# Attention scores from two 32 bit parts, two heads side by side in the array

## The chip, the core and the metric

The kernel runs on one core of a Trainium2 chip. The metric is the device time of one execution in microseconds (us). A core has a matrix engine (TensorE, PE in the profile, with its weight loads as PEld), a vector engine (VectorE, DVE), a scalar engine (ScalarE, ACT), a general engine (GpSimd, POOL), and DMA queues, which SyncE (SP) and ScalarE issue to here. Every engine works through its own instructions in order and waits for others by semaphores. TensorE writes to eight PSUM banks of 128 rows of 512 32 bit words; VectorE and ScalarE read them there.

## The reference

One transformer block on 2048 tokens of width 512: a layer norm with scale and shift from a condition vector, attention, a gated residual, a second layer norm, an MLP of width 1792 with GELU, a gated residual. The attention has 32 heads of width 16 and works on four segments of 512 tokens. Inside a segment it is causal softmax attention; beside that, a linear memory carried over the segments is read. Cut to the part that the change touches:

```python
logits = jnp.einsum("bhqd,bhkd->bhqk", qs, ks) * scale + mask   # scale 1/4, mask -1e9 above the diagonal
p = _softmax(logits, axis=-1)
a_dot = jnp.einsum("bhqk,bhkd->bhqd", p, vs)
...
o = g * a_mem + (1.0 - g) * a_dot
```

q and k are scaled such that the logits are large, so the maximum of a row has to be subtracted before the exponential, and the products need more than bf16 accuracy.

## The kernel before

The program has three stages. First the projections of q, k and v and the memory, for all four segments; then the scores, with the output projection and the second layer norm mixed in; then the MLP. An explicit order fixes every engine's sequence.

**Operands of the scores.** `proj` (L488) splits q and k, each 128 x 512 for eight heads, into three bf16 parts, and `store` writes them to DRAM as six terms: the six products of parts that matter. `load_stacks` (L177) brings four heads (a *quartet* Q of 32) back as `qst` and `kst`, 96 rows (six terms of 16 dimensions) x 4 heads x 512 positions. One product over 96 rows then gives a score to nearly 32 bit accuracy. Four pairs of buffers rotate (`NK`).

**Two passes over the scores.** A step P handles one pair of heads (64 steps, two per quartet).
- S (`s_part`, L624): scores with queries in rows, for the maxima, in blocks i = 3, 2, 1, 0 of 128 queries with 512, 384, 256 and 128 keys. Parts S0 and S1 take two single banks each, one per head, and `masked_max` (L618, a custom VectorE instruction) adds the causal mask and takes the maximum. S2 and S3 put both heads in one bank; for the last block the mask is added by a product with an identity (`s_mask`, L658, token M3) and one reduction (L622) takes both heads' maxima. S runs four steps (`LEAD`) ahead of T.
- `m_rows` (L671, GpSimd) splits a quartet's negative maxima into three bf16 parts, `m_put` (L677) transposes them on PE (L679) into the bank `mm`, copies them out on ACT and writes them with one DMA, issued by ACT, as rows 96 to 98 of `qst`; `kst` has ones there.
- T (`st_part`, L706): scores transposed, keys in rows, over 99 rows (L700), so that the maximum is already subtracted; ACT takes the exponential from PSUM to `pt` (L715, L726), GpSimd cuts above the diagonal (`causal`, L703). T0 to T3 take a bank per head, T4 and T5 one for both.
- `pv_part` (L740): the values' product, four heads in four 32-column strips of the array, once per key block j for a quartet.

**Order.** The rows of `PRM['order']` give a step's sequence, one row for even and one for odd steps of each segment. S0 to S3, M3 and T0 to T5 are the parts above; c0 to c9 are slots, and a table (`ap`, position 10 x step + slot) puts everything else there: loads of stacks (`stacks`), `m_rows`, `m_put`, value products (`pv`), output projection (`wo_part`, L817), its residual and the layer norm. Six single banks `att` are handed out in turn; one bank is `pv`, one `mm`.

## Time and profile before

| | us |
|---|---|
| median of three runs | 805.82 (804.58 to 812.59) |
| the profiled execution | 803.54 |
| its span | 801.8 |
| granted TensorE clock, mean | 0.994 |

| line | what | count | busy us |
|---|---|---|---|
| L611 | S products, parts 0 to 2 | 384 | 94.3 |
| L700 | T products | 512 | 106.8 |
| L740 | value products | 992 records | 88.2 |
| L618 | masked maxima on DVE | 384 | 192.3 |
| L622 | maxima by reduction on DVE | 64 | 27.2 |
| L715, L726 | exponentials on ACT | 384 | 183.3 |
| L703 | causal cuts on POOL | 256 | 101.9 |

Busy time of a group is the time in which at least one of its instructions ran. PE's records overlap, since a product's end is modelled and the next starts before it; what a product costs in a row of products is the distance of starts, which the chain of work gives. The score stage lasts from about 185 to 490 us of the span.

### The profile page before, as it was taken

To read this page: it belongs to the slowest core of one execution; us is meant where nothing else is said; L and a number is where in the kernel's file an instruction comes from. 1 tells how busy PE (TensorE), PEld (TensorE's weight loads), DVE (VectorE), ACT (ScalarE), POOL (GpSimd) and SP (SyncE) were. 2 spreads that over 40 slices of the span, in tenths; PEclk is the share of its full clock that TensorE was granted. 3 is DMA by queue.
4 is the path that set the end of the run, shared out by engine and by line. 5 is a ranking of instruction groups with operands and counts; after the bars stand their busy time and mean duration, and the time that the engine had idled before them with its cause. 6 is when DMAs were issued, how large, how long until landed. Compare 5 with 4: busy or idle time off the path is not lost.

```text
span 801.8 us, 14163 instructions
## 1 busy us (share of the span) xinstructions
PE 782.6 (98%) x4585; PEld 532.0 (66%) x4585; DVE 557.9 (70%) x1411; ACT 464.9 (58%) x912; POOL 336.2 (42%) x556
## 2 busy tenths in 40 slices
PE   9999999999999999999999998989999999999998
PEld 4877777876444455445544555768888888888887
DVE  6686697459888877697778779866659866533423
ACT  3465545465778766675678574757745336653221
POOL 1347366451478555567866586133000404400000
PEclk9999999999999999999999999999999999999999
DMA  9597857495565676768557854584575644445443
GB/s 339 183 318 233 284 181 233 149 331 170 147 195 164 187 209 174 219 179 216 155 175 203 233 160 147 173 283 155 192 255 176 195 136 158 158 145 171 156 134 117
DMA packets 108818, 156.10 MB, mean 195 GB/s; under 512 B 16324, under 2 KB 55620, under 8 KB 108744
## 3 DMA queue, kind: packets, MB, share of 16 engines
q1 hardware_dynamic: 106248, 153.23, 60.7%
q10 hardware_dynamic: 2496, 1.97, 0.8%
q8 instruction: 36, 0.59, 0.3%
q14 instruction: 38, 0.31, 0.1%
HBM read 93.95 MB, written 60.83 MB: 193 GB/s over the span
## 4 chain that ended last, share of the span: by engine, by line
PE 76%; ACT 7%; DMA 6%; DVE 6%; issue 3%; POOL 1%; SPq 1%; ACTq 0%; DVEq 0%; POOLq 0%
PE pv L740 8%; PE bx L1059 7%; PE att L700 7%; PE att L611 6%; PE q L318 5%; PE bx L1324 5%; PE by L1324 4%; PE bv L1324 4%; PE k L318 4%; PE mm L817 4%; PE bv L1059 4%; PE v L469 3%; DMA qst<-ms 2%; PE spare L1324 2%; ACT pt L715 2%
## 5 line engine op out<-in xcount | busy, mean ns | idle before, releaser
L618 DVE CUSTOM_DVE_ANT_0 dump<-att,maskb 128x512 bf16<-128x512 f32 (+2 forms) x384 | 192.3, 553 | 27.0 <-PE att L611 24.8
L715 ACT ACTIVATE pt<-att 128x512 f32<-128x512 f32 (+1 forms) x256 | 126.1, 558 | 47.0 <-PE att L700 44.3
L703 POOL TENSOR_SCALAR_AFFINE_SELECT pt<-pt 128x256 f32<-128x256 f32 x256 | 101.9, 416 | 82.5 <-ACT pt L715 51.6
L700 PE MATMUL att<-qst,kst 99*128 99x512 bf16 (+3 forms) x512 | 106.8, 301 | 5.6 <-DMA qst<-ms 3.5
L611 PE MATMUL att<-kst,qst 96*128 96x512 bf16 (+2 forms) x384 | 94.3, 327 | 1.7 <-DMA qst<-QD 1.4
L740 PE MATMUL pv<-pt,V 128*32 128x512 f32 (+2 forms) x992 | 88.2, 446 | 0.0
L854 POOL TENSOR_TENSOR wb<-wa 128x256 f32<-128x256 f32 x24 | 21.0, 876 | 154.9 <-DMA wa<-in_w 148.9
L700 PEld LDWEIGHTS <-kst 99*128 99x128 bf16 x512 | 42.9, 97 | 57.6 <-issue 38.7
L726 ACT ACTIVATE pt<-att 128x512 f32<-128x512 f32 (+1 forms) x128 | 57.2, 514 | 21.6 <-PE att L611 19.6
L611 PEld LDWEIGHTS <-qst 96*128 96x128 bf16 x384 | 33.2, 98 | 40.7 <-issue 23.8
L141 DVE TENSOR_TENSOR gl<-s,gh 128x512 fp32r<-128x512 f32 x34 | 24.5, 721 | 42.0 <-ACT gh L138 42.0
L138 ACT ACTIVATE gh<-s 128x512 fp32r<-128x512 f32 x34 | 21.3, 628 | 47.2 <-PE spare L1324 17.1
L740 PEld LDWEIGHTS pv<-pt,V 128*32 128x32 f32 x992 | 22.1, 108 | 36.4 <-issue 26.1
L622 DVE TENSOR_REDUCE nm<-att 128x2 f32<-128x256 f32 x64 | 27.2, 425 | 22.1 <-PE att L658 17.7
L1064 ACT ACTIVATE s<-s,b1t 128x512 f32<-128x512 f32 x42 | 30.2, 720 | 18.6 <-DVE s L1068 18.6
L1068 DVE TENSOR_TENSOR s<-bv,s 128x512 f32<-128x512 f32 x28 | 19.2, 688 | 25.5 <-PE bv L1059 20.2
L618 DVE DVE_READ_ACCUMULATOR2_ANT nm<- 128x1 f32 x384 | 31.9, 83 | 0.0
L514 POOL TENSOR_TENSOR q<-qr,q 128x512 bf16<-128x512 f32 x16 | 18.7, 1167 | 26.7 <-ACT q L513 26.3
L505 POOL TENSOR_SCALAR qp<-qp 128x512 f32<-128x512 f32 x12 | 19.1, 1594 | 24.0 <-ACT qp L500 24.0
L141 DVE TENSOR_TENSOR w1ml<-s,w1mh 128x512 fp32r<-128x512 f32 x18 | 13.0, 721 | 21.5 <-ACT w1mh L138 21.5
L318 PE MATMUL q<-Ahh,wqh 128*128 128x512 f32 x64 | 25.9, 405 | 0.4 <-DVE Ahh L140 0.4
L138 ACT ACTIVATE w1mh<-s 128x512 fp32r<-128x512 f32 x18 | 11.3, 628 | 25.6 <-PE spare L1324 13.1
(364 smaller groups left out, 2112.7 us busy)
## 6 DMA issues: line engine op xcount, KB each, us to landing
GD<-s SPq DMA_DIRECT2D x56, 256.0 KB
s<-GD SPq DMA_DIRECT2D x52, 256.0 KB
kst<-KD SPq DMA_DIRECT2D x32, 384.0 KB
qst<-QD SPq DMA_DIRECT2D x32, 384.0 KB
TD<-ts SPq DMA_DIRECT2D x32, 256.0 KB
xt<-X2D SPq DMA_DIRECT2D x28, 256.0 KB
wa<-in_w SPq DMA_DIRECT2D x28, 256.0 KB
QD<-q SPq DMA_DIRECT2D x16, 384.0 KB
```

Source lines behind the costliest of these rows:

```text
L138: act.activation(hi, src, AF.Copy)
L141: lo_eng.tensor_tensor(out=lo, in0=src, in1=hi.bitcast(F32), op=ALU.subtract)
L318: pe.matmul(ps, a[:, k, 128 * g:128 * g + 128], b[k], start=(k == 0 and i == 0), stop=(k == KB - 1 and i == 2))
L611: pe.matmul(ps, q_of(P, h, i), k_of(P, h, 128 * (i + 1)), start=True, stop=True)
L618: v.tensor_tensor_reduce(out=dump[n_dump[0] % 2][:, :n], in0=src, in1=maskb[:, 512 - n:], scale=-1.0, scalar=-4 * NEG, op0=ALU.add, op1=AL ...
L700: pe.matmul(ps, k[:99, e, 128 * j:128 * j + 128], q[:99, e, 128 * j:512], start=True, stop=True)
L703: pool.affine_select(out=t, in_=t, pattern=pattern, compare_op=ALU.is_ge, fill=0.0, base=0, channel_multiplier=-1)
L715: act.activation(pt[:, h, :], ps[:, :n], AF.Exp, scale=0.25)
L726: act.activation(pt, pv_, AF.Exp, scale=0.25)
L740: pe.matmul(ps[32 * c:32 * c + 32, lo:hi], V[4 * s + j][:, VW * hd:VW * hd + 32], pt[:, c % 2, lo - o:hi - o], start=start, stop=stop)
L1059: pe.matmul(ps, a[:, i, k, :], b[k], start=start and k == 0 and c == 0, stop=k == 1 and c == 2, skip_group_check=not start)
L1324: pe.matmul(ps, a[:, c], w[:, lo:hi], start=(f == 0 and i == 0), stop=(last and i == 2))
```

## The change

- **Operands.** q and k are split into two 32 bit parts (type `float32r`) in place of three bf16 parts; three terms in place of six, 48 rows per head. The bytes in DRAM stay. A head of a pair stands in rows 0 to 47 or 64 to 111 of `qst` and `kst` (now 128 x 2 x 512), its three maxima in the rows behind (48 to 50, 112 to 114). `load_stacks` issues four DMAs per quartet in place of two, `m_put` two in place of one.
- **Banks.** Three pairs of banks `att` in place of six single ones; one head of the pair writes to each bank. A step takes six turns: three S parts (blocks 3; 2 and 0; 1) and three T parts (blocks 0; 1 and 3; 2).
- **Mask.** All blocks get the mask by products: for each head two products over 64 rows, each adding the mask for 64 of the 128 queries (`hid`, `hmask`). The custom maximum is gone; a plain reduction takes both heads at once.
- **Exponentials** run over both heads and both banks: 1024, 1024 and 512 columns.
- **Order.** One sequence for all steps; loads of stacks four slots later; output projection in other slots. In the first stage, a copy on ACT and a subtraction on GpSimd per projection fall away.

```diff
-PRM = {'order': ['S0 c0 c1 T0 T1 S1 c2 T2 c3 c4 c5 T3 S3 c6 M3 S2 c7 c8 c9 T4 T5',
-           'T0 S0 c0 c1 c2 S1 c3 T2 T3 T1 S2 c4 c5 T4 S3 M3 T5 c6 c7 c8 c9',
...
+ORDER = 'S0 T0 S1 c0 c1 c2 c3 c4 T1 S2 c5 c6 c7 c8 c9 T2'
...
- 'stacks': -64,
+ 'stacks': -60,
...
- 'wo': [[2, 10, 10, 10], [6, 10, 11, 11], [2, 10, 10, 11]],
+ 'wo': [[2, 6, 10, 10], [2, 6, 10, 10], [2, 6, 10, 10]],
...
+    TERMS = {"q": (slice(0, 3, 2), slice(1, 2)), "k": (slice(0, 2), slice(2, 3))}
...
-            d[i] = (pl or wmp).tile([128, 4, 512], BF16, **a)
+            d[i] = (pl or wmp).tile([128, 2, 512], F32R, **a)
...
-            sp.dma_start(st[:96], dd[s][g].rearrange("c r e n -> (c r) e n")[:, 4 * t:4 * t + 4, :])
+            for h in range(2):
+                e = 4 * t + 2 * h
+                sp.dma_start(st[64 * h:64 * h + 48].bitcast(F32), dd[s][g].rearrange("c r e n -> (c r) e n")[:, e:e + 2, :])
...
+    v.memset(hid, 0.0)
+    v.memset(hmask, NEG)
+    for t, op, fill in ((hid, ALU.not_equal, 1.0), (hmask, ALU.is_gt, 0.0)):
+        for h in range(2):
+            r = slice(64 * h, 64 * h + 64)
+            pool.affine_select(out=t[r], in_=t[r], pattern=[[-64, 2], [1, 128]], compare_op=op, fill=fill,
+                               base=0, channel_multiplier=-1)
...
-            v.tensor_tensor(out=r1, in0=ps, in1=parts[0], op=ALU.subtract)
+            v.tensor_tensor(out=parts[1], in0=ps, in1=parts[0].bitcast(F32), op=ALU.subtract)
...
-            act.activation(parts[1], r1, AF.Copy)
-            pool.tensor_tensor(out=parts[2], in0=r1, in1=parts[1], op=ALU.subtract)
...
-                 for n, c in (("att", 6), ("pv", 1))}
+                 for n, c, d in (("att", 3, [2, 512]), ("pv", 1, [512]))}
...
+        SP_, TP = ((3,), (2, 0), (1,)), ((0,), (1, 3), (2,))
...
+            ps, lo = bank("att"), 0
+            for c, i in enumerate(SP_[part]):
                 n = 128 * (i + 1)
                 for h in range(2):
+                    pe.matmul(ps[:, h, lo:lo + n], q_of(P, h, i), k_of(P, h, n), start=c == 0, stop=False,
+                              skip_group_check=True)
+                lo += n
+            w = 128 * len(SP_[part])
+            o = lo - 128 if w == 128 else 256
+            for a in range(2):
                 for h in range(2):
+                    r = slice(64 * h, 64 * h + 64)
+                    dst, m = ps[:, h, o:o + w], hmask[r, a]
...
+                    pe.matmul(dst, hid[r, a], m, start=False, stop=a == 1, skip_group_check=True)
+            lo = 0
+            for i in SP_[part]:
                 n = 128 * (i + 1)
+                v.tensor_reduce(out=nms[Q][:, 0:8:4, 4 * p + i], in_=ps[:, :, lo:lo + n], axis=AX.X, op=ALU.max,
+                                negate=True)
+                lo += n
...
         def q_of(P, h, i):
-            return qst[P // 2 % NK][:96, 2 * (P % 2) + h, 128 * i:128 * i + 128]
+            return qst[P // 2 % NK][64 * h:64 * h + 48, P % 2, 128 * i:128 * i + 128]
...
+            ms = sb.tile([64, 128], F32R, tag="ms", bufs=2, name=f"ms{Q}")
+            copy(PRM["mse"], ms, mm[:64, :128])
+            for h in range(2):
+                act.dma_start(qst[Q % NK][64 * h + 48:64 * h + 51].bitcast(F32), ms[32 * h:32 * h + 24].bitcast(F32))
...
         def st_part(P, part):
+            js = TP[part]
+            w = 256 if part == 2 else 512
             ps = bank("att")
+            pt = late[0].tile([128, 2, w], F32, tag=f"pt{part}", bufs=(3, 4, 4)[part], name=f"pt{P}_{part}")
+            lo = 0
+            for j in js:
                 n = 512 - 128 * j
                 for h in range(2):
+                    st_mm(ps[:, h, lo:lo + n], P, h, j)
+                pts[P, j] = pt[:, :, lo:lo + n]
+                lo += n
+            act.activation(pt, ps[:, :, :w], AF.Exp, scale=0.25)
+            for j in js:
+                causal(pts[P, j][:, :, 0:128], [[0, 2], [1, 128]])
```

How the order moves, at two places. First PE in the second segment, from a quartet's transposition of maxima (L679 before, L650 now, from `nm`) to the S products of the next step. Tiles carry a number; `att` are the banks. Before:

```order
L679 MATMUL mm<-identb,nm_2056 128x128
L700 LDWEIGHTS kst_1838
L700 MATMUL att_2063<-qst_1837,kst_1838 128x256 [waits DVE_49]
...
L700 MATMUL att_2064<-qst_1837,kst_1838 128x128 [waits DVE_49]
...
L700 MATMUL att_2065<-qst_1837,kst_1838 128x512 [waits Activation_49]
L611 LDWEIGHTS qst_2138
L611 MATMUL att_2066<-kst_2139,qst_2138 128x512 [waits Activation_49]
```

The change:

```order
L650 MATMUL mm<-identb,nm_1910 128x128
L672 MATMUL att_1919<-qst_1714,kst_1715 128x256 [waits DVE_49]
...
L616 MATMUL att_1917<-kst_1939,qst_1938 128x512 [waits Activation_49]
...
L672 MATMUL att_1918<-qst_1714,kst_1715 128x512 [waits DVE_49]
...
L616 MATMUL att_1919<-kst_1939,qst_1938 128x384 [waits Activation_49]
```

The banks now return after three turns: the last row, S1 of the next step, takes the pair 1919 that T2 took in the second row, and waits for ACT to have read it.

Second, ACT at the same kind of place, around the copy of the maxima (`ms`). Before:

```order
L715 ACTIVATE pt_1_4170<-att_2066 128x384 [waits PE_49]
L132 ACTIVATE ms_4193<-mm 48x128 [waits DMAHW4_49,PE_49]
L682 DMA qst_2075<-ms_4193 3x16x128 [waits DMAHW3_49,Activation_49]
L726 ACTIVATE pt_2_4196<-att_2063 128x512 [waits DVE_49,PE_49]
L726 ACTIVATE pt_3_4201<-att_2064 128x256 [waits DVE_49,PE_49]
```

The change:

```order
L691 ACTIVATE pt_1_4656<-att_1917 128x1024 [waits DVE_49,PE_49]
L124 ACTIVATE ms_4674<-mm 64x128 [waits DMAHW0_49,PE_49]
L654 DMA qst_1721<-ms_4674 3x8x128 [waits DMAHW6_49,Activation_49]
L654 DMA qst_1721<-ms_4674 3x8x128 [waits DMAHW1_49]
L691 ACTIVATE pt_2_4679<-att_1919 128x512 [waits PE_49]
```

Between the exponentials of two T parts stand now a copy and two DMA issues, where one issue stood.

128 lines of the change are left out of this document (34 added, 94 removed), and 8 rows, old and new, of the table PRM.

## The prediction

> **What bounds the kernel now.** I read the page first: the busy line, to see which engine has no time left.
>
> ```profile
> span 801.8 us, 14163 instructions
> PE 782.6 (98%) x4585; PEld 532.0 (66%) x4585; DVE 557.9 (70%) x1411; ACT 464.9 (58%) x912; POOL 336.2 (42%) x556
> ```
>
> TensorE (PE) is covered for 98% of the span. An average hides stages, so the second view was the busy time by stretches, and for the score stage the same view for line L648 alone, which runs once per step (a step is one pair of heads, 64 in all).
>
> ```profile
> 60.00:100.00 40.00, 40.00 (x181) 29.58 (x180) 25.41 (x47) 21.55 (x40) 21.84 (x18) 1.00 0.76 259
> ...
> 200.00:240.00 40.00, 38.88 (x324) 16.85 (x324) 33.84 (x133) 31.69 (x72) 24.09 (x55) 1.00 0.59 169
> 280.00:320.00 40.00, 39.84 (x310) 21.03 (x308) 29.72 (x110) 25.85 (x59) 21.19 (x48) 1.00 0.70 198
> 200.00:240.00 40.00, 2.21 (x10) 0.98 (x10) 1.00 0.59 169
> 280.00:320.00 40.00, 1.77 (x8) 0.79 (x8) 1.00 0.70 198
> ```
>
> The columns are the engines in the page's order (PE, PEld, DVE, ACT, POOL), then clock, DMA share, GB/s; the last two rows have PE and PEld of L648 only. Ten steps in 40 us are 4.0 us per step, eight (where output projections are mixed in) 5.0. PE is full in both, so the projections before (60 to 100) and the score stage alike are paced by PE's own work. The third view, the chain of work that ended last, gives that work piece by piece.
>
> ```profile
> 408.96 0.22 PE att L611 x2
> ...
> 410.20 0.43 PE att L611 x2
> ...
> 411.70 0.33 PE att L611 x2
> 412.03 1.00 PE pv L740 x8
> 413.03 0.27 PE att L700
> 413.30 0.06 PE att L648
> 413.35 0.06 PE att L649
> 413.41 0.11 PE att L658
> ...
> 417.19 0.35 PE pv L740 x8
> ```
>
> Two score products of 512 columns take 0.43 us, of 384 0.33, of 256 0.22, one of 128 0.055 (two from 413.30 to 413.41), the mask 0.11. A step's maxima part (S) is 0.43 + 0.33 + 0.22 + 0.11 + 0.11 = 1.20 us, its transposed part (T) the same without the mask, 1.09: together 2.29.
>
> **1. Shorter score products: -44 us.** S and T keep their columns, but the two heads of a pair now stand in rows 0 to 63 and 64 to 127 and go to different banks. The trace has no such pair of row halves. What it has is four column strips: the value product of 512 columns (L740, x8) issues for four heads, two records each, in 1.00 us, where a single record is 619 ns long.
>
> ```profile
> L740 PE MATMUL pv<-pt,V 128*32 128x512 f32 x248 | 33.9, 619 | 0.0
> 780.42 0.39 PE L1324 MATMUL bv<-w2h,gh 128*128 128x512 f32 x1
> 780.65 0.39 PE L1324 MATMUL bv<-w2h,gl 128*128 128x512 f32 x1
> 781.10 0.28 PE L1324 MATMUL mm<-w2h,gh 128*128 128x256 f32 x1
> 781.22 0.28 PE L1324 MATMUL mm<-w2h,gl 128*128 128x256 f32 x1
> ```
>
> So strips do run beside each other, and I take row halves to do the same; at worst they gain nothing (a rival below). The new operands are 32 bits wide, of the kind of L1324: such products start 0.23 us apart at 512 columns and 0.12 at 256, nearly the bf16 pace. I estimate 0.175 at 384 and 0.06 at 128 from these (128 was not seen: between 0.06 and the 0.23 of 512). A pair then costs one product: T = 0.23 + 0.175 + 0.12 + 0.06 = 0.585. S has that and twelve mask products per step in six pairs, four of 128 and two of 256 columns: 4 x 0.055 + 2 x 0.11 = 0.44, so 1.025. Sum 1.61, 0.68 less per step, 44 us in 64 steps. The Trainium skill, "TensorE: Matmul & The Clock Gate", Part 3, says that products in distinct row groups run concurrently, and gives 3.07x for four of 32 rows; no run here shows row groups, and by it the term stands.
>
> **2. Changes of array shape: +10 us.** L740 costs 1.00 us at 512 columns and 0.35 at 128: 0.65 for 384 columns, so 0.87 for 512 and 0.13 to 0.15 on top per visit. I read that as the price of going into strips and out. Visits to strips stay as many. But now the row halves are a shape of their own, so the max transposition (32 times, m_put) and the output projections (36 groups) each add one: 68 x 0.145 = 10. Bounds 0 and 20 (both ways).
>
> **3. Banks wait for ScalarE: +83 us.** This is what decides. Before, six single banks rotate; after, three pairs, each held until one instruction over both heads has read it. S waits for the exponential (ACT) of the T part three turns earlier, T for the maximum (DVE) of an S part. In ScalarE's queue stands, once per quartet, m_put: a copy and now two DMA issues, ahead of the exponential of T2, and the next step's S1 needs T2's banks.
>
> ```profile
> L715 ACT ACTIVATE pt<-att 128x512 f32<-128x512 f32 x128 | 74.5, 616 | 19.1 <-PE att L700 17.0 <-PE att L611 2.1
> L715 ACT ACTIVATE pt<-att 128x384 f32<-128x384 f32 x128 | 59.4, 500 | 27.9 <-PE att L700 27.3
> L132 ACT ACTIVATE ms<-mm 48x128 bf16<-48x128 f32 x31 | 8.3, 267 | 1.5 <-PE mm L679 0.6
> L682 ACTq DMA_DIRECT2D qst<-ms x32: 728/729/1353, 192.0 to 470.3; - x32
> L611 PE MATMUL att<-kst,qst 96*128 96x512 bf16 x128 | 38.5, 380 | 1.5 <-DMA qst<-QD 1.4
> 222.96 3.40 DMA qst<-ms
> 444.28 0.05 issue
> 226.41 0.61 PE L700 MATMUL att<-qst,kst 99*128 99x512 bf16 x2 [0.35 <-DMA qst<-ms]
> ```
>
> 116 ns per 128 columns make the 1024-wide exponential 0.616 + 4 x 0.116 = 1.08 us, T2's 512 0.62; one issue holds ACT 0.73; a product's result is out 0.17 us after the next may start (0.38 against 0.215), and a hand-off takes some 0.04 (an estimate from gaps in the chain like that at 444.28). For quartets 8 to 23, from the end of T1 on PE: ACT has exponential T1 done at 0.21 + 1.08 = 1.29, copy 1.56, two issues 3.05, exponential T2 3.67, banks free 3.71. PE meanwhile does S2 (0.23), the transposition with its change of shape (0.21) and T2 (0.12): 0.56. S0 waits for T1's banks until 1.33 (stall 0.77), then S0 0.34 and T0 0.23, and S1 stands at 1.90 until 3.71: stall 1.81. Together 2.58 x 16 = 41 us. In quartets 24 to 31 a value product (1.00) lies between, m_put comes at 1.29, ACT frees the banks at 1.29 + 0.21 + 0.27 + 0.03 + 1.46 + 0.62 + 0.04 = 3.92, PE is there at 1.98: 1.94 x 8 = 16. In quartets 0 to 7 m_put comes less than a step ahead of its reader, T0: the second DMA lands 0.51 + 0.73 + 3.40 = 4.64 later. PE's work until T0 is value products of 384 and 128 columns in one visit (1.0), T1 0.23, S2 0.23, T2 0.12, S0 0.34 and the wait of 0.98 below: 2.9. The wait of 1.7 stands against 0.35 now (the row at 226.41), +1.35 x 8 = 11. In each quartet's step without m_put, S0 still waits for exponential T1: 1.33 - 0.35 = 0.98 where nothing lies between, 0.3 where output products (3 x 0.23) do, half of quartets 8 to 31 each: 12 x 0.98 + 12 x 0.3 = 15. Sum 41 + 16 + 11 + 15 = 83. What is least known is the issue: other DMAs on this queue took 0.39.
>
> ```profile
> L233 ACTq DMA_DIRECT2D wm<-in_wmod x4: 334/392/458, 3.4 to 5.2; - x4
> L622 DVE TENSOR_REDUCE nm<-att 128x2 f32<-128x256 f32 x61 | 25.9, 425 | 21.3 <-PE att L658 17.0 <-ACT pt L715 2.1
> L618 DVE CUSTOM_DVE_ANT_0 dump<-att,maskb 128x512 bf16<-128x512 f32 x120 | 78.0, 687 | 5.5 <-PE att L611 3.9 <-POOL pt L703 1.5
> L618 DVE CUSTOM_DVE_ANT_0 dump<-att,maskb 128x384 bf16<-128x384 f32 x120 | 62.0, 554 | 20.8 <-PE att L611 20.2
> ```
>
> At 0.39 for each of the two the stalls of 24 quartets shrink by 0.68, 16 us; I keep 0.73, since the new DMA has the old one's shape, three rows cut in blocks.
>
> **4. Costed at nothing.** VectorE: 133 ns per 128 columns, 425 for 256, make the four reductions 1.22 + 0.96 + 0.69 + 0.425 = 3.30 us per step, under the step's length; it binds only if PE's work and waits fell below 3.3. The causal cuts on GpSimd are as many as before. The projection stage loses a copy on ACT and a subtraction on GpSimd, beside a PE with 40.00 of 40 busy: at most -1. Loads of the stacks are four instead of two, of the same bytes, issued four slots later: about two steps (9 to 11 us) less 1.1 ahead of their reader, against the longest landing on the chain:
>
> ```profile
> 436.48 7.80 DMA qst<-QD
> ```
>
> They stay covered while steps last over 4.8; without cover up to 1 us per quartet, 0 to +30. I take 0, PE having waited 1.4 us in all for these (row of L611 above).
>
> **Sum**: -44 + 10 + 83 = +49, on the profiled execution's own 803.54 us (its span and 1.7 us around it): 852.5, say 853. The median of the runs shown is 2.3 us above that execution, within their spread.
>
> **Rivals.** (a) *Weight loads set the pace.* A pair needs two loads.
>
> ```profile
> L700 PEld LDWEIGHTS <-kst 99*128 99x128 bf16 x512 | 42.9, 97 | 57.6 <-issue 38.7 <-DMA qst<-ms 6.1
> L318 PEld LDWEIGHTS q<-Ahh,wql 128*128 128x128 f32 x64 | 12.0, 188 | 2.2
> ```
>
> A 32 bit load is 91 ns longer than a bf16 one, and L1324 at 256 columns shows it fits in 0.12. If two loads run one after the other, no pair takes under about 0.21: T = 0.23 + 3 x 0.21 = 0.86, S 1.30, so the first term is -9 instead of -44, and the stalls shrink by some 9: 803.5 - 9 + 10 + 74 = 878. The Trainium skill, same page, "LDWEIGHTS" and "Weight-path perf modes", gives 128 columns / 1.2 = 107 ns and no fast load for 32 bit weights; by that estimate two loads are 0.21 as well. For it: half the columns' time, the same number of loads. Against: loads may run beside each other in separate rows. 20%.
> (b) *The halves don't run side by side*, so the change doesn't do what it says: S 2 x 0.585 + 0.88 = 2.05, T 1.17, 3.22 per step, +0.93 x 64 = 60; PE's own work then covers about half the stalls: 803.5 + 60 + 10 + 42 = 915. The strips of L740 speak against it. 15%.
> (c) *Faster: the stalls behind m_put don't form.* Place: S1 after T2. Terms 1 and 2 leave -34 us, 1.06 per quartet; if the waits of a quartet sum to less than that, the kernel is faster. That needs the two issues to hold ACT for well under 0.4 in all. At half a microsecond per quartet it is 803.5 - 34 + 16 = 786. For it only the shorter issues of L233. 12%.
> (d) *Half the stalls*: 803.5 - 34 + 42 = 811. 8%.
>
> **How the numbers follow.** The forecast (828 to 868) has 45%, (a) 20, (b) 15, (c) 12, (d) 8. About 1% (8 us) is what a measurement of this kernel can tell from no change. The range 800 to 905 leaves out (c) and half of (b), 20%. Faster by over 1%: 0.12; within 1%: 0.06, the larger part of (d); slower 0.82.
>
> **What would show it.** After: PE's busy share in the score stage well under today's, with ScalarE's exponentials as the releaser of the maxima products; two DMA issues of 0.73 ahead of T2's exponential; a step of 4.6 to 5.6 us. Step 1 is right if the second head's product starts within some 0.02 us of the first; at 0.1 it is (a), at 0.2 (b). The prediction is wrong if PE stays full in that stage (then (a) or (b), or, with shorter steps, (c)), or if VectorE is what PE waits for.

## The result and the profile after

The changed kernel took 905.0 us in the median (896.9 to 920.8), the kernel before 806.4 beside it: a ratio of 1.117, interval [1.107, 1.128]. It is slower, as forecast, but by 98 us where the prediction had 49; 905 is the very end of its range. One of the four executions (920.8 us, at a granted clock of 0.918) and, further below, two each of `r6_fill_half` and `r10_rows64` ran slower than their fellows, and ratios and the table of the experiments leave them out. The trace read below is that of another execution of the changed kernel, of 916.2 us; the three timed ones counted ran at a granted clock of 0.940 to 0.950 and this one at 0.927, so it shows the same picture some ten microseconds stronger.

First the page: span, busy time, and the rows of PE and of its granted clock in 40 slices.

```profile
span 914.5 us, 14721 instructions
PE 840.6 (92%) x5289; PEld 574.1 (63%) x5289; DVE 535.1 (59%) x836; ACT 436.5 (48%) x688; POOL 299.5 (33%) x527
PE   9999999898887889888898888889999999999998
PEclk9999999997878997966787799989999999999999
```

Two things changed in the slices of the score stage: PE is no longer full, and its clock is no longer 9. The busy time by stretches gives both a size (columns PE, PEld, DVE, ACT, POOL, then clock, DMA share, GB/s). Before, over the score stage, up to the first product of the MLP (490.4 there, 606.0 after):

```profile
184.00:490.40 306.40, 298.48 (x2368) 150.39 (x2367) 247.35 (x890) 217.56 (x486) 193.82 (x392) 0.99 0.63 183
```

After, over the three stages:

```profile
0.00:187.00 187.00, 182.06 (x890) 136.15 (x890) 118.69 (x232) 79.70 (x139) 52.00 (x80) 1.00 0.73 255
187.00:606.00 419.00, 358.28 (x3043) 191.79 (x3042) 232.11 (x322) 209.96 (x295) 196.85 (x392) 0.85 0.50 132
606.00:914.50 308.50, 300.28 (x1359) 246.14 (x1357) 184.30 (x284) 146.84 (x255) 50.67 (x56) 0.99 0.53 173
```

The score stage went from 306.4 to 419 us, +113; the two others add up to nothing (+3 and -3). Inside it PE stands idle 419 - 358.3 = 60.7 us against 7.9: **+53 by waiting**. The clock is 0.85 against 0.99: it stood at 0.50 for 130 of the 419 us, which is 65 us of missing clock, against 2 before: **+63 by clock** (an upper bound, since some of it falls into the waits). The rest, 113 - 53 - 63 = **-3, is PE's own work**, with the waits in it that PE's modelled ends hide (below). The prediction had +83, nothing and -34.

The waits are where it put them. The waits view (us in total, times, longest), of PE and, last, of its weight loads:

```profile
PE att L616 <- ACT pt L691: 48.9, 52, 1.7
PE att L672 <- DVE nm L632: 3.6, 9, 0.5
PEld att L616 <- ACT pt L691: 70.6, 77, 2.0
```

The weight loads of S wait 22 us longer than its products: PE counts as busy to the modelled end of the product before. S1 starts 0.47 us after T0's second product (median at full clock), whose own pitch is 0.235, so some of these 22 us are waits that stand under "own work".

And one quartet of the second segment in the chain of work, from T1 to the next S1 (start, length, what):

```profile
320.53 0.45 PE att L672 x4
...
321.93 0.27 ACT ms L124
...
322.21 0.73 ACTq L654
322.94 0.04 issue
322.98 0.73 ACTq L654
...
323.81 0.61 ACT pt L691
...
324.46 0.51 PE att L616 x4
```

After T1 (320.53) and its exponential comes ScalarE's queue as predicted: copy 0.27, two issues of 0.73, T2's exponential 0.61, and only then S1's four products. The same place in the timeline shows both stalls in brackets:

```profile
322.08 0.50 PE L616 MATMUL att<-kst,qst 48*128 48x512 f32 x2 [0.35 <-ACT pt L691]
...
324.46 0.51 PE L616 MATMUL att<-kst,qst 48*128 48x384 f32 x4 [1.46 <-ACT pt L691]
```

S0 stalls 0.35, S1 1.46; the prediction had 0.77 and 1.81. VectorE, costed at nothing, is next to nothing: 3.6 us in the waits.

The clock was in no step of the prediction. In windows of 2 us (time, PE busy first, clock third from the end) it stands at 1.00 or at 0.50 and little between:

```profile
249.00:251.00 2.00, 0.35 (x1) 0.18 (x1) 0.53 (x1) 1.93 (x3) 0.77 (x3) 1.00 0.73 127
251.00:253.00 2.00, 0.87 (x8) 0.75 (x9) 0.00 (x0) 0.00 (x0) 0.41 (x1) 0.52 0.02 5
253.00:255.00 2.00, 2.00 (x15) 1.38 (x13) 1.43 (x2) 1.10 (x2) 0.01 (x1) 0.50 0.62 144
...
261.00:263.00 2.00, 2.00 (x31) 0.94 (x23) 0.91 (x2) 0.48 (x2) 1.45 (x2) 0.92 0.14 54
```

After a stretch in which PE stood idle for 2.8 of 4 us, it runs at half clock for some ten microseconds, and from 253 on it is full there.

### The profile page after: what moved, and what is told of

It is laid out like the page before. It is cut to its first block, busy times and chain, and to the rows that moved or that the text cites. A ratio compares the mean times of both kernels' runs of the same rounds, so it can differ in the third digit from the quotient of the medians.

```text
span 918.9 us, 14721 instructions
## 1 busy us (share of the span) xinstructions
PE 849.3 (92%) x5289; PEld 577.5 (63%) x5289; DVE 537.2 (58%) x836; ACT 436.5 (48%) x688; POOL 299.5 (33%) x527
## 4 chain that ended last, share of the span: by engine, by line
PE 78%; ACT 6%; DMA 5%; ACTq 4%; DVE 3%; issue 3%; SPq 0%; POOL 0%; DVEq 0%
PE pv L706 11%; PE bx L1024 7%; PE att L672 6%; PE att L616 5%; PE mm L783 5%; PE bx L1289 5%; PE q L317 4%; PE by L1289 4%; PE bv L1289 4%; PE k L317 4%; ACTq L654 4%; ACT pt L691 4%; PE v L468 4%; PE bv L1024 3%; PE att L628 3%
## 5 line engine op out<-in xcount | busy, mean ns | idle before, releaser
L632 DVE TENSOR_REDUCE nm<-att 128x2 f32<-128x1024 f32 (+3 forms) x256 | 201.5, 821 | 184.5 <-PE att L628 160.9
L691 ACT ACTIVATE pt<-att 128x1024 f32<-128x1024 f32 (+1 forms) x192 | 166.2, 882 | 181.5 <-PE att L672 160.6
L616 PE MATMUL att<-kst,qst 48*128 48x512 f32 (+3 forms) x512 | 96.5, 405 | 52.3 <-ACT pt L691 47.6
L672 PE MATMUL att<-qst,kst 51*128 51x512 f32 (+3 forms) x512 | 100.1, 421 | 4.8 <-DVE nm L632 4.0
L616 PEld LDWEIGHTS att<-kst,qst 48*128 48x128 f32 x512 | 55.8, 221 | 77.6 <-ACT pt L691 69.0
L672 PEld LDWEIGHTS att<-qst,kst 51*128 51x128 f32 x512 | 51.8, 213 | 56.3 <-DVE nm L632 29.8
L628 PE MATMUL att<-hmask,hid 64*128 64x128 bf16 (+1 forms) x768 | 74.9, 270 | 0.0
L628 PEld LDWEIGHTS <-hid 64*128 64x128 bf16 x768 | 27.4, 108 | 17.4 <-issue 8.3
L783 PE MATMUL mm<-woh,oh 128*128 128x512 f32 x52 | 26.9, 517 | 0.0
L317 PE MATMUL q<-Ahl,wqh 128*128 128x512 f32 x64 | 25.6, 400 | 0.0
```

Source lines behind the costliest of these rows:

```text
L317: pe.matmul(ps, a[:, k, 128 * g:128 * g + 128], b[k], start=(k == 0 and i == 0), stop=(k == KB - 1 and i == 2))
L616: pe.matmul(ps[:, h, lo:lo + n], q_of(P, h, i), k_of(P, h, n), start=c == 0, stop=False, skip_group_check=True)
L628: pe.matmul(dst, hid[r, a], m, start=False, stop=a == 1, skip_group_check=True)
L632: v.tensor_reduce(out=nms[Q][:, 0:8:4, 4 * p + i], in_=ps[:, :, lo:lo + n], axis=AX.X, op=ALU.max, negate=True)
L672: pe.matmul(ps, k[r, P % 2, 128 * j:128 * j + 128], q[r, P % 2, 128 * j:512], start=True, stop=True, skip_group_check=True)
L691: act.activation(pt, ps[:, :, :w], AF.Exp, scale=0.25)
```

## The experiments

Three questions: are the waits those of ScalarE's queue and the three pairs of banks; what do pairs of row halves cost; and what halves the clock. Two theories of the clock: *idle gaps* alone, or *use*, the share of the array's rows that work times the share of time. All ratios are to the kernel before, on the same chip; score stages start at 187 us and are taken up to the first product of the MLP.

| run | median us | ratio [interval] | clocks |
|---|---|---|---|
| r1_dma_sp | 879.4 | 1.094 [1.088, 1.099] | 0.950 to 0.957 |
| r2_t2_first | 862.6 | 1.076 [1.066, 1.087] | 0.950 to 0.964 |
| r3_fill | 886.9 | 1.104 [1.100, 1.107] | 0.965 to 0.969 |
| r4_before_two | 953.6 | 1.185 [1.179, 1.191] | 0.912 to 0.924 |
| r4b_split | 814.3 | 1.014 [1.008, 1.019] | 0.994 to 0.997 |
| r6_fill_half | 892.3 | 1.111 [1.100, 1.122] | 0.954, 0.965 |
| r10_rows64 | 901.8 | 1.122 [1.120, 1.125] | 0.950, 0.950 |
| r7b_order | 847.1 | 1.054 [1.049, 1.059] | 0.954 to 0.964 |
| r9_dve_mask | 835.4 | 1.041 [1.038, 1.045] | 0.942 to 0.946 |
| r14_fill | 866.5 | 1.080 [1.076, 1.085] | 0.955 to 0.961 |
| r15_rows64 | 829.0 | 1.032 [1.030, 1.035] | 0.962 to 0.964 |

**The changed kernel once more** (`after_again`), unaltered.

> The changed kernel unaltered, profiled once more, for a trace at a usual granted clock. Theory (idle gaps of TensorE lower the granted clock, and the pairs of row halves save nothing): about 897 to 906 us, busy time of PE in the score stage at least 0.08 us idle per us, granted clock there 0.85 to 0.95, and every 5 us stretch either at 1.00 or at 0.50. Rival (the low clock of the first profile was a disturbance of that one execution): the clock near 0.99 and the time under 880.

It took 916.2 us at 0.927, ten over the theory's range, with 0.85 in the stage and 0.145 us idle per us. The low clock is the kernel's own and no accident of one execution. That every 5 us lie wholly at 1.00 or 0.50 was too strong: the clock of this trace changes in steps of 3.41 us.

### The waits for ScalarE

**The maxima's DMAs issued by SyncE** (`r1_dma_sp`).

```diff
-                act.dma_start(qst[Q % NK][64 * h + 48:64 * h + 51].bitcast(F32), ...)
+                sp.dma_start(qst[Q % NK][64 * h + 48:64 * h + 51].bitcast(F32), ...)
```

> The change, with m_put's two DMAs issued by SyncE instead of ScalarE, so that ScalarE goes from the copy straight to T2's exponential. Queue theory (the stalls at S1 come from the two issues of 0.73 us ahead of that exponential): PE's waits for ACT at L616, 117 us in the changed kernel's trace (69.0 + 47.6, PE and its weight loads), fall to under half, and 24 x 1.46 = 35 us go. Gap theory of the clock (granted clock 0.83 in the score stage because PE stands idle): it rises to over 0.92 too and the time is 835 to 860 us. Shape theory of the clock (products over 48 rows count as little work, whatever the gaps): clock stays at 0.80 to 0.87, time 865 to 880. If the issues are not the cause: within 1% of the changed kernel, 895 to 915.

It is 76 us slower than the kernel before instead of 98. Its waits:

```profile
PE att L672 <- DMA qst<-ms: 22.9, 13, 4.4
PE att L616 <- ACT pt L691: 14.4, 29, 1.3
```

S's wait for ScalarE went from 48.9 to 14.4 us, so the issues were its main part. But on SyncE's queue the DMAs stand behind others (in 15 of 32 quartets the first is issued 0.35 to 4.9 us after the copy, on ScalarE's it was 0.03 each time), and T now waits 22.9 us for them: most of what was saved turned into a new wait. The clock in the stage (187 to 568 us) is 0.91, between the two theories of the clock, and the time, 879, lies in the range of the shape theory.

**T2 two slots earlier** (`r2_t2_first`), so that its exponential stands ahead of the copy and the issues.

```diff
-ORDER = 'S0 T0 S1 c0 c1 c2 c3 c4 T1 S2 c5 c6 c7 c8 c9 T2'
+ORDER = 'S0 T0 S1 c0 c1 c2 c3 c4 T1 S2 c5 c6 c7 T2 c8 c9'
```

> The change, with the token T2 moved ahead of slots c8 and c9 in the step's sequence, so that T2's exponential stands ahead of m_put's copy and issues on ScalarE, which still issues both DMAs. Queue theory: the 1.5 to 1.8 us stall at S1 goes in 24 quartets, S0's stays: -36 to -43 us at an equal clock; with the gap theory of the clock on top, 835 to 860 us, and clock in the score stage over 0.92. Shape theory: clock unchanged, 860 to 875. If holding ScalarE as such is the cost (not its place in the queue): no gain, 895 to 915.

862.6 us, +59 instead of +98: some 40 us come back by a place in the order alone, 3 short of the range. The wait at L616 fell to 21.4 us, and the clock in the stage (187 to 551 us) is 0.92.

**One more issue in the kernel before.** First `r4_before_two`, the one DMA issued twice.

```diff
-            act.dma_start(qst[Q % NK][96:99], ms)
+            for _ in range(2):
+                act.dma_start(qst[Q % NK][96:99], ms)
```

> The kernel before, with m_put's DMA issued twice (same data to the same rows), so that ScalarE is held by 0.73 us more per quartet, as in the change, but with six single banks. If it is the rotation of three pairs that turns ScalarE's hold into a PE stall: +0 to +8 us. If ScalarE's time is the bound as such: 32 x 0.73 = 23 us or more.

This run misfired. Both DMAs write the same rows, and the second is issued only when the first has landed, with ScalarE behind it:

```profile
309.57 2.37 DMA qst<-ms
...
312.01 0.73 ACTq L683
```

From 309.57 to 312.74 it holds ScalarE 3.2 us in place of 0.73, and says nothing of one more issue. It says something of the clock, though, to which I return.

Then `r4b_split`, with two issues to different rows.

```diff
-            act.dma_start(qst[Q % NK][96:99], ms)
+            act.dma_start(qst[Q % NK][96:97], ms[:16])
+            act.dma_start(qst[Q % NK][97:99], ms[16:48])
```

> The kernel before with the DMA of the maxima as two issues to different rows, so that ScalarE is held 0.73 us longer per quartet, with the six single banks as they were. Theory (the second issue hurts the changed kernel because three pairs of banks leave no slack): six banks absorb it, +0 to +8 us (ratio 1.000 to 1.010), PE's waits for ACT at the maxima products under 10 us. Rival (an issue of 0.73 on ScalarE costs its length in any rotation): +23 us, 1.03.

+9 us in the medians (ratio 1.014), just above the theory's 0 to 8 and far from the rival's 23. PE's waits for ACT are 2.1 us at the maxima products, none before, and 5.3 at T's, 1.7 before. So six single banks absorb most of a second issue, and do not stall where the three pairs do.

**Another order, nothing else** (`r7b_order`): different sequences for even and odd steps, with other work between each T part and the S part that takes its banks.

```diff
-ORDER = 'S0 T0 S1 c0 c1 c2 c3 c4 T1 S2 c5 c6 c7 c8 c9 T2'
+ORDER = ('c0 S2 c1 T1 c2 T2 c3 c4 c5 T0 S0 S1 c6 c7 c8 c9',
+         'c0 c1 c2 c3 T2 S1 T1 c4 c5 S0 T0 S2 c6 c7 c8 c9')
```

> The changed kernel with another order alone, different for even and odd steps, so that other work stands between a T part and the S part that takes its banks; mask products and DMAs as changed. If the waits for ScalarE are what the order makes them: PE's waits for ACT at the maxima products fall from about 120 to under 30 us and the time to 835 to 860 us, the clock still at 0.95 to 0.97, since the pairs use half of the array as before. If the waits move elsewhere: 870 to 900 us.

847.1 us, inside the theory's 835 to 860, with a wait of

```profile
PE att L617 <- ACT pt L692: 8.9, 13, 2.0
```

in place of 48.9. So 54 us of the 98 hang on the order, by the waits and by the clock that they cost; what is left, +44, is there with hardly any wait for ScalarE. In the stage (187 to 539.1 us) PE still stands idle 27 us, 14 of them for VectorE, and 34 us of clock are missing (0.90): against the kernel before that is +19 and +32.

### What pairs of row halves cost

**Pairs in a row of their like** (`r5_rates`): a block ahead of the first stage, 16 pairs of each kind, operands of ones. For 512 columns:

```python
for _ in range(16):
    for h in range(2):
        pe.matmul(rp[h], rz[64 * h:64 * h + 48, :128], rz[64 * h:64 * h + 48, :512], start=True, stop=True)
```

> The changed kernel with an extra block in the first stage: 16 pairs of each kind on two banks, with nothing between them, operands of constants. Left as it is otherwise; its time is not compared. What the pitch of a pair of 48-row halves with 32 bit operands is, by the prediction: 512 columns 0.23, 384 0.175, 256 0.12, 128 0.06 us. Rival (a), two weight loads one after the other: 0.23, 0.21, 0.21, 0.21. Halves not concurrent: 0.46, 0.35, 0.24, 0.12. From the trace of the changed kernel I now expect between: 0.28 to 0.30, 0.21 to 0.24, 0.17, 0.13. bf16 pairs (two 64-row halves): 0.23, 0.12, 0.06 by the prediction, with a fast load; 0.24, 0.16, 0.10 if the second load still costs. Same half twice: 0.46 at 512, 0.2 at 128. Full array and 48 rows in turn, 256 columns: 0.24 per two products if a change of rows costs nothing, 0.4 if it drains the array.

One line each for 32 bit pairs of 512, 384, 256 and 128 columns and bf16 pairs of 256 and 128 (durations, then first and last start):

```profile
L291 PE MATMUL rp<-rz x32: 383/390/501, 8.1 to 11.7; 48*128 48x512 f32 x32
L294 PE MATMUL rp<-rz x32: 330/331/343, 11.9 to 14.6; 48*128 48x384 f32 x32
L297 PE MATMUL rp<-rz x32: 275/280/280, 14.7 to 16.5; 48*128 48x256 f32 x32
L300 PE MATMUL rp<-rz x32: 221/271/277, 16.6 to 18.3; 48*128 48x128 f32 x32
L312 PE MATMUL rp<-rb x32: 269/269/279, 42.1 to 44.1; 64*128 64x256 bf16 x32
L315 PE MATMUL rp<-rb x32: 216/216/227, 43.9 to 45.0; 64*128 64x128 bf16 x32
...
47.13 0.38 PE L317 MATMUL rq<-rz 48*128 48x256 f32 x1
47.44 0.28 PE L318 MATMUL rq<-rb 128*128 128x256 bf16 x1
```

From one block's first start to the next, by 16: about 0.235, 0.175, 0.12 and 0.11 us per 32 bit pair, and 0.11 for bf16 of 256 columns; bf16 pairs of 128 start 0.055 apart in the middle of their row (0.07 in the mean of it). The last rows are 48 rows and the full array in bf16 in turn, 256 columns each: a round takes 0.53 where the parts make 0.23, so there and back costs 0.30, more than the 0.4 per round that I had for a drained array. The other blocks (the same half twice, bf16 pairs of 512) ran at half clock wholly or in part and give no pitch. The halves run side by side and the prediction's pitch holds at 512, 384 and 256 columns; at 128 it is 0.11 with 32 bits, not 0.06. My later reading of 0.28 to 0.30 from the changed kernel, and rival (a)'s 0.21, are both out.

**Pairs in turn with something else** (`r11_switch`), twelve rounds of each kind.

```python
for _ in range(12):
    for h in range(2):
        pe.matmul(rp[h][:, :256], rz[64 * h:64 * h + 48, :128], rz[64 * h:64 * h + 48, :256], start=True, stop=True)
    pe.matmul(rq[0][:, :256], rz[:128, :128], rz[:128, :256], start=True, stop=True)
```

> The changed kernel with an extra block in the first stage; otherwise as it is, its time is not compared. Twelve rounds each of a pair of 32 bit halves (256 columns, 0.12 us in a row of its like) with something else in turn: bf16 halves (0.11), 32 bit halves of 51 rows (0.12), the full array in 32 bits (0.12), four strips (0.5 with their own change), and for comparison the full array with strips and bf16 with 32 bits in the full array. Theory (the missing 0.47 us per step goes into a change between groups of products, some nine of them per step): a round with bf16 halves takes 0.30 to 0.36, with 51 rows 0.24 to 0.27, with the full array 0.45 to 0.53. Rival (the pairs are slow in the score stage for another reason, such as other work on the banks): every round takes the sum of its parts to 0.02. Then 40 products each over 96, 80 and 64 rows, dense, 32 bits, 512 columns, each after 20 over 128 rows: if the granted clock follows how many rows work, 64 rows run at 0.5 and 96 at 1.0; if it follows only idle time, all run at 1.0.

The end of the rounds of 48 and 51 rows and the first of halves and full array in the timeline:

```profile
17.20 0.28 PE L300 MATMUL rp<-rz 51*128 51x256 f32 x2
17.32 0.28 PE L303 MATMUL rp<-rz 48*128 48x256 f32 x2
17.53 0.38 PE L304 MATMUL rq<-rz 128*128 128x256 f32 x1
17.84 0.38 PE L303 MATMUL rp<-rz 48*128 48x256 f32 x2
```

48 and 51 rows alternate at 0.12 (17.20 to 17.32), and a round with bf16 halves takes 0.25, the sum of its parts (0.23) to 0.02: there the rival was right. But a round with the full array takes 0.63 for 0.12 + 0.12, so there and back costs 0.39 here, and the round is beyond even my 0.45 to 0.53. Strips in turn with halves ran at half clock, so that part says nothing of price. In this run 96, 80 and 64 rows, dense, all ran at full clock, so the 0.5 I expected at 64 rows was wrong.

In the kernel itself a change costs less. Around a transposition of maxima in `after_again`, at full clock:

```profile
320.97 0.29 PE L628 MATMUL att<-hmask,hid 64*128 64x128 bf16 x4
321.19 0.23 PE L650 MATMUL mm<-identb,nm 128*128 128x128 bf16 x1
321.35 0.38 PE L672 MATMUL att<-qst,kst 51*128 51x256 f32 x2
```

The transposition starts 0.148 after the last mask pair (321.04) and T2 0.16 after the transposition, where their own pitches are 0.066 and 0.058: 0.18 there and back, the same in all 16 quartets with this sequence except two. Behind an output projection the next product starts 0.32 after the last one, 0.24 before the change: 0.08 to 0.09.

### What halves the clock

**Idle gaps alone can do it.** In the misfired `r4_before_two` all score products use 96 or 99 rows and none stands in a half:

```profile
214.00:216.00 2.00, 1.25 (x16) 0.65 (x15) 1.62 (x9) 0.10 (x1) 0.00 (x0) 1.00 0.03 6
216.00:218.00 2.00, 1.34 (x5) 0.52 (x5) 0.67 (x3) 2.00 (x5) 0.82 (x2) 0.81 0.03 6
218.00:220.00 2.00, 2.00 (x9) 0.61 (x11) 1.41 (x7) 1.64 (x5) 1.57 (x5) 0.50 0.74 197
```

Idle for 1.4 of 4 us, then half clock. The Trainium skill, "TensorE: Matmul & The Clock Gate", Part 1 and "Why this matters for your kernels", tells of a monitor of PE's activity with windows of about 3.4 us and asks for no idle gap over some 3 us. This trace agrees on the half clock (0.50) and differs on the gap: 1.4 us in 4, the longest gap 1.2, were enough.

**Added work** (`r3_fill`): five full-array bf16 products of no use between T0 and S1 in odd steps.

```diff
+            for _ in range(5):
+                pe.matmul(mm, identb, wol_b, start=True, stop=True)
```

> The change, plus five idle products (bf16, full array, 128x512, into the bank mm, results unused) between T0 and S1 of every odd step from 15 to 61, that is 24 x 1.1 us of added PE work, placed where PE waits 1.5 us for ScalarE. Nothing that is computed depends on them. Gap theory of the clock: granted clock in the score stage rises from 0.83 to over 0.92 and the time falls to 850 to 885 us although work is added. Shape theory: clock within 0.03 of the changed kernel's, time 895 to 925.

+83 us instead of +98, with about 26 us of work more: S's wait for ScalarE went from 48.9 to 23.2 us, the clock up to 0.965 to 0.969 (0.93 in the stage). The gap theory had the clock right and the time 2 us too low. With fillers of 48 rows of one half (`r6_fill_half`, `q_of(P, 0, 0)` and `k_of(P, 0, 512)` as operands):

> As the run with five filling products per two steps, but each filler has 48 rows of one half (32 bit, 512 columns) in place of the full array in bf16. It adds the same idle work in the same place. Theory (the clock follows how long TensorE stands idle): as with full-array fillers, clock about 0.965, 885 to 890 us. Rival (the clock follows how much of the array works, so half-array work does not count or counts against it): clock at or under 0.945, 905 to 925 us.

The two executions counted took 886.7 us at 0.965 and 898.0 at 0.954: one as the theory has it, one between the two. Inconclusive.

**Groups with a wait behind each** (`r12_duty`): N products, then a wait until ScalarE has read the bank.

```python
for _ in range(10):
    for _ in range(8):
        pe.matmul(rq[0][:, :512], rz[:128, :128], rz[:128, :512], start=True, stop=True)
    act.activation(ro, rq[0], AF.Copy)
```

> The changed kernel with an extra block in the first stage; otherwise as it is, its time is not compared. Groups of 24, 16, 12, 8 and 4 products over 128 rows (32 bits, 512 columns), each group followed by a wait until ScalarE has read the bank (about 0.9 us idle); then groups of 24, 16 and 8 pairs of 48-row halves in the same way; ahead of each kind 20 dense products. Busy shares of about 0.86, 0.80, 0.75, 0.67 and 0.5. Theory (idle gaps of 1 to 2 us alone lower the clock where they sum to 15 to 20% of the time): 24 stays at 1.00, 16 or 12 falls in part, 8 and 4 run at 0.5. Rival (only rows count, gaps of a microsecond do not): the full array stays at 1.00 throughout, and only the pairs of halves fall.

Groups of 8 over 128 rows; of 4, earlier and later:

```profile
109.00:138.00 29.00, 21.53 (x84) 14.54 (x83) 0.00 (x0) 5.69 (x10) 0.00 (x0) 1.00 0.00 0
142.40:160.00 17.60, 10.90 (x38) 6.15 (x36) 0.00 (x0) 5.37 (x9) 0.00 (x0) 1.00 0.00 0
165.00:171.80 6.80, 4.67 (x10) 2.47 (x9) 0.00 (x0) 1.74 (x3) 0.00 (x0) 0.50 0.00 0
```

Groups of 24 to 8 stay at full clock, even though a quarter of the time is idle with 8 (theory: half clock), and 4 fell after some 20 us. The pairs of halves stayed at full clock down to groups of 8, against the rival. So an even idle share of a quarter is borne, more than the 15% of the score stage; but the stalls there come bunched, 2.8 us in 4, and this run doesn't excuse those.

**Rows and idle share apart** (`r13_use`), with dense products over k rows, then groups as above.

```python
for _ in range(80):
    pe.matmul(rq[0][:, :512], rz[:48, :128], rz[:48, :512], start=True, stop=True)
```

> The changed kernel with an extra block in the first stage; otherwise as it is, its time is not compared. Ahead of each part 60 dense products over 128 rows. Parts: 80 dense products over 64, 56, 48 and 32 rows (32 bits, 512 columns); 80 over 128 rows with 64 columns of weights; 30 rounds of four strips; then groups with a wait of about 0.9 us behind each: over 128 rows 6, 4 and 3 products, over 96 rows 8, over 64 rows 16 and 8. Use is the share of rows times the share of time that products run: 0.5, 0.44, 0.375, 0.25; then 0.60, 0.50, 0.43 for the groups over 128 rows; 0.50 for 96 rows, 0.40 and 0.33 for 64. Theory (the granted clock halves where use falls under about one half): full at 64 rows dense, half at 48 and 32, half for 128 rows by 4 and 3, and half for 64 rows by 16 and 8, though their idle share (0.2, 0.33) is one that 128 rows bear at full clock. Rival (idle time alone): all dense parts full, 64 rows by 16 and 8 full, 128 rows by 4 and 3 half.

Dense over 64, 56 and 48 rows; then groups over 128 rows of 6, 4 and 3, and over 64 rows of 16 and of 8:

```profile
20.40:38.40 18.00, 18.00 (x80) 14.61 (x80) 0.00 (x0) 0.00 (x0) 0.00 (x0) 1.00 0.10 30
51.80:69.80 18.00, 18.00 (x80) 14.62 (x80) 0.00 (x0) 0.00 (x0) 0.00 (x0) 1.00 0.00 0
86.00:114.00 28.00, 28.00 (x69) 21.45 (x68) 0.00 (x0) 0.00 (x0) 0.00 (x0) 0.51 0.00 0
...
230.50:268.50 38.00, 26.58 (x98) 16.95 (x97) 0.00 (x0) 9.13 (x16) 0.00 (x0) 1.00 0.00 0
300.00:320.00 20.00, 14.42 (x29) 8.11 (x28) 0.00 (x0) 4.18 (x7) 0.00 (x0) 0.50 0.00 0
350.20:387.00 36.80, 21.12 (x68) 10.78 (x67) 0.00 (x0) 12.54 (x21) 0.00 (x0) 1.00 0.00 0
...
470.00:520.50 50.50, 46.01 (x104) 32.25 (x102) 0.00 (x0) 3.58 (x6) 0.00 (x0) 0.50 0.00 0
560.00:597.00 37.00, 30.75 (x67) 20.09 (x66) 0.00 (x0) 4.78 (x8) 0.00 (x0) 0.50 0.00 0
```

PE without a moment's idle falls to half clock over 48 rows (and over 32) and not over 56. Groups of 16 over 64 rows, idle a fifth of the time at full clock (16 x 0.23 against 0.9), fall to half, while groups of 6 over 128 rows, idle for 11.4 of 38 us, stay at full. Full too stayed groups of 8 over 96 rows, and dense 128 rows with 64 columns of weights or in four strips. So rows count as well as time: **use** decides, and idle time is one way to lose it. One row seems to go against it: groups of 3 over 128 rows, with the least use of those three, stayed at full clock where groups of 4 did not.

The traces settle it if use is counted step by step. The clock changes in steps of 3.41 us in each of them. As an estimate, let each product hold its rows of 128 for 0.215 us per 512 columns (two take 0.43 in the chain before), twice that at half clock and again twice in a strip (eight take 1.00), at most 1 in all. Over the 17 traces whose full clock is 1.00 (all but `r10_rows64`'s), of the steps at full clock with use under 0.36 the next one is at half clock in 225 of 248 cases; with use from 0.42 on in 1 of 3688; between, in 23 of 147. Time alone sorts worse: where PE is covered for 0.5 to 0.8 of the step, 173 of 455 fall. At half clock the way back is longer: 141 of 144 steps with use over 0.78 are followed by full clock, 6 of 220 under 0.7. Groups of 3 stand at 0.38 in each step, in the band between. Groups of 4 waver, and fell behind a step that took in two waits and stood at 0.38 as well: in this band the count does not tell which fall.

**The same in the score stage.** `r10_rows64` has T over 64 rows in place of 51, the rows more holding zeros.

```diff
-slice(64 * h, 64 * h + 51)
+slice(64 * h, 64 * h + 64)
```

> The changed kernel with the transposed score products over 64 rows per head in place of 51, the 13 rows more holding zeros, so the same result. Their columns, and so their time at one clock, stay. Theory (the clock follows idle gaps alone): nothing changes, 895 to 917 us at 0.93 to 0.95. Rival (it follows how many of the 128 rows work): clock 0.96 or more, 870 to 890 us.

The two executions at 0.950 took 900.9 and 902.6 us, as the changed kernel itself: nothing gained. The theory of use expected a gain here, and it was not there. Counted as above there was little to gain: in `after_again` 18 of the 19 falls of the clock follow a step with use under 0.36, and with 64 rows for T's 51 it would still be under 0.36 in 16 of them.

`r9_dve_mask` keeps operands and halves, but puts the masked maximum back on VectorE in place of the mask products, with an order of its own.

```diff
-                    pe.matmul(dst, hid[r, a], m, start=False, stop=a == 1, skip_group_check=True)
+                    masked_max(nms[Q][:, 4 * h, 4 * p + i:4 * p + i + 1], ps[:, h, lo:lo + n], n)
...
+ORDER = ('c0 c1 T0 c2 S1 T1 c3 c4 c5 c6 c7 c8 S2 S0 c9 T2',
+         'c0 c1 c2 c3 S2 T2 S0 c4 c5 c6 T0 c7 S1 T1 c8 c9')
```

> A version meant to beat the changed kernel: operands in two 32 bit parts and heads in row halves as changed, but the masked maximum of the kernel before on VectorE per head and block in place of the twelve mask products, and another order for even and odd steps in which other work stands between a T part and the S part that takes its banks. VectorE needs about 3.9 us per step for it. If the pairs' cost and the stalls are as I now read them: 0.45 us of mask products and most of the 1.5 us stalls per quartet go, clock 0.98 or more, 795 to 815 us. If PE's idle time comes from something else: 850 to 880 us.

835.4 us, the best version with the reference's scores, still 4.1% behind the kernel before and in neither of my ranges: the clock stayed at 0.945 where I had put 0.98. `r15_rows64` is this version with all score products over 64 rows:

> The version with the masked maximum on VectorE, with all score products over 64 rows per head in place of 48 and 51, and the exponentials with a factor of 0 (the rows more hold old maxima, so the scores are not the reference's; the columns, the products and the waits stay). At one clock its time is that version's. Theory (use of the array): the pairs go from 0.75 to 1.0 of the rows, some 0.3 us of use per step of 4.4; clock from 0.945 to 0.965 or more, 815 to 825 us. Rival (idle time alone): 832 to 840 us at 0.945.

From 187 to 540 us, the version and the version over 64 rows:

```profile
187.00:540.00 353.00, 318.21 (x2329) 165.16 (x2328) 261.76 (x1081) 213.77 (x305) 200.98 (x395) 0.87 0.61 163
```

```profile
187.00:540.00 353.00, 313.73 (x2357) 167.30 (x2356) 268.62 (x1094) 218.88 (x316) 204.03 (x399) 0.92 0.62 165
```

PE's idle time is 35 us in the one and 39 in the other, and yet the clock is 0.87 in the first and 0.92 in the second; the time falls from 835.4 to 829.0, with ratios whose intervals don't meet. It is the direction of the theory of use, and less than its 815 to 825. The exponentials are all 1 in this run, and they are operands of the value products: that the clock follows the values is a rival that this comparison does not exclude.

`r14_fill` adds six full-array products per two steps to `r9_dve_mask`.

> The version with the masked maximum on VectorE, with six idle products over the full array (bf16, 512 columns, 1.3 us) per two steps added. They add 39 us of work to an engine that stands idle some 35 us in that stage. Theory (use of the array): use rises by 0.65 us per step of 4.4, the clock to 0.98 or more, and the 45 us of lost clock come back against at most 39 us of work: 800 to 835 us. If the clock in that version has another cause: 850 to 875 us at 0.945.

866.5 us at 0.955 to 0.961: the clock rose, and the time with it, by 31 us for some 37 of added work (29 steps x 6 x 0.215). The theory's 800 to 835 missed; the time lies in the other range, whose unchanged clock it did not keep. Filling pays only where PE would have waited anyway, as in `r3_fill`.

## Why the prediction was wrong

The sign and the mechanism on which it decided hold; the size was off by 52 us. That 905 still lies at the end of the range is no merit: the range reached so far for rival (b), which did not happen.

- **Bound before:** right. PE was full, and the score stage is where the time went, all of the +113 in the spans compared.
- **Term 1, -44:** mis-sized. Three of four pitches were right (0.235, 0.175, 0.12), 128 columns were not (0.11 for 0.06), nor were the mask pairs: in the stage they start 0.066 and 0.118 apart and make 4 x 0.066 + 2 x 0.118 = 0.50 for 0.44. T is 0.64, S 0.64 + 0.50 = 1.14, together 1.78 for 1.61: the term is (2.29 - 1.78) x 64 = -33. In S1 and T1, 384 and 128 columns behind each other take 0.33 in the stage, not 0.285, which takes another 6 us from the gain: about -27.
- **Term 2, +10:** about right. The 0.39 of `r11_switch` would make it 68 x 0.39 = 27, but the stage shows 0.18 per transposition and some 0.09 per output projection: 32 x 0.18 + 36 x 0.09 = 9. Terms 1 and 2 are then -18; the -3 found as own work contains a part of the 22 us of hidden waits.
- **Term 3, +83:** right in place, cause and order of magnitude: two issues of 0.73 ahead of T2's exponential, S1 and S0 stalled. The stalls are 1.46 and 0.35 where it had 1.81 and 0.77, and idle time rose by 53, more with the hidden part. Moving T2 (`r2_t2_first`) or the whole order (`r7b_order`) takes some 40 and 54 us off, clock included.
- **Term 4:** right. VectorE, the cuts on GpSimd and the first stage cost next to nothing (3.6 us of waits for VectorE, +3 in the first stage); S waited 1.1 us for the stacks.
- **The step that failed is the sum itself:** it counted every product at full clock. The clock, 0.994 before, was 0.940 to 0.950 in the timed executions after: (1 - 0.945) x 902 = 50 us of missing clock against 5, an upper bound as above. These 45 are most of the 52 by which the forecast fell short. In the traces it is 63 by clock; the own work, 31 more than put, and the waits, 30 less, cancel.

Of what would show it, the waits and the two issues came true, and so did the second head's start: in 454 of 506 pairs of `after_again` it is within 0.02 us of the first. A step of 4.6 to 5.6 us did not: it took 419 / 64 = 6.5 in the mean, half clock included. Rivals (a) and (b) are out by `r5_rates`, though (b)'s 915 came nearest to the time. Rivals (c) and (d) needed shorter stalls.

What is shown: the waits and their cause, the pairs' pitch, and that the clock follows use, step by step, in every trace with a full clock of 1.00. Use is rows times time, so no single share of the 50 us belongs to either. But a pair uses 96 or 102 of the 128 rows, as one product did before (96 or 99): against the kernel before it is the time in which products run that fell, by the waits and by the shorter work. What is argued: what would bring the rest back. The other order, with hardly a wait left for ScalarE, still ran at 0.96, and more rows (`r15_rows64`) gave 6 us, with other values in the products.

## What to carry to other kernels

Two products in the row halves of the array do run at the price of one, but an array that does its work in less time is an array less used, and if nothing takes up the time won, the clock may halve; count what the engine does per microsecond before counting on its clock. When banks are handed out in larger units, look in each reader's queue for what stands ahead of the instruction that frees them, and move that, before anything else: here a place in the order was worth 40 to 54 us. A block of a few dozen products settles a pitch that a trace of overlapping records leaves open, but what a change of shape costs has to be read in the kernel: the block gave 0.30 and 0.39 us, the kernel 0.18.

## What the runs showed of the hardware

- TensorE's granted clock is 1.00 or 0.50 in 17 traces (0.85 or 0.50 in that of `r10_rows64`) and changes in steps of 3.41 us. In the changed kernel's score stage it stays at half for 3.4 to 13.7 us at a time.
- Whether it falls follows the use of the array in the step before (rows times time, counted as above): 225 of 248 steps under 0.36 are followed by half clock, 1 of 3688 from 0.42 on; it comes back after 141 of 144 steps over 0.78. Dense 32 bit products over 48 rows of 128 run at half clock, over 56 rows at full (operands of ones).
- Pairs of 48-row halves with 32 bit operands: 0.235 us at 512 columns, 0.175 at 384, 0.12 at 256, and 0.11 at 128. Between 32 bit and bf16 halves a change is nearly free (0.02 a round); between halves and the full array it is 0.39 there and back in 32 bits and 0.30 with a full array in bf16, in rows of such rounds, and 0.18 around the transposition in the kernel.
- One DMA issue of three rows in blocks holds ScalarE 0.73 us.
